# One store of the result from every 16th partition, behind the closing barriers of a decode kernel

## The chip, the cores and the metric

The kernel runs on one core of a Trainium2 chip. The metric is the time of one execution on the device, in microseconds (us). It is given as the median of three runs, and one more execution, which the hardware profiler recorded, gives the trace. The trace has the core's engines: TensorE (PE, and PEld for its weight loads), VectorE (DVE), ScalarE (ACT), GpSimd (POOL) and SyncE (SP), and 16 DMA engines that carry all transfers between HBM and the on-chip memory.

## What is computed

The kernel mixes two branches for two tokens (batch 2, one position each, model width 512). Branch A is attention of one new position over the last 4,096 positions of a cache, with 32 query heads that share 8 key and value heads of width 128. Branch B is a dense layer of 1,792 units with the Mish activation. A sigmoid gate weighs the two.

```python
W = min(4096, max(256, Sk // 4))                       # 4096
q = (x @ wq).reshape(B, Sq, Hq, Dh)                    # 2 tokens, 32 heads of 128
scores = einsum("bhqd,bhkd->bhqk", q, k[last W]) * Dh ** -0.5
a = einsum("bhqk,bhkd->bhqd", softmax(scores), v[last W]).reshape(B, Sq, Hq * Dh) @ wo
h = x @ w1 + b1
b = (h * tanh(softplus(h))) @ w2
g = sigmoid((x * gate_w).sum(-1, keepdims=True))
return g * a + (1 - g) * b                             # (2, 1, 512), float32
```

All inputs and the output are float32.

## The kernel before

Everything is read once: the query weights (two loads of 4 MB), `w1`, then for each of the 8 key heads a block of keys and a block of values (4 MB each), then `w2` and `wo` in pieces. All loads are issued from SP's queue, in one fixed order; the big ones take turns in five buffers of the pool `stream`, so that a load waits until the buffer of the fifth load before it is free.

With only two tokens, a plain matrix product would use two rows of the output. The kernel instead divides the 128 partitions of a PSUM tile into 4 blocks of `Q = 32` rows. The inputs of a matmul are padded to 32 columns (`x32`, `oT`, `actT`: the two tokens are columns 0 and 1, the other 30 are zero), and block `j` of the output takes another slice of the weights. So a result tile holds, in partition `32 * j + b`, slice `j` of token `b`; the other partitions hold zeros.

- `queries` (from line 107) makes the queries of four key heads each, transposes them, and copies the two tokens' columns into `qz` (16 copies, listed in the profile under line 122).
- `hidden` (line 202) makes the hidden layer, adds the bias while it reads the transposed tile (line 227), and writes the activations, weighted by one minus the gate, into the token columns of `actT` (line 242).
- `softmax` and `values` (lines 126 and 145) go over the key heads; `weights` and `outputs` (lines 158 and 193) scale what the heads gave and write it into the token columns of `oT` (line 198).
- `project` and `finish` (lines 276 and 285) multiply by `wo` and `w2`. The last sum is in the PSUM tile `fin`, of 128 x 128: partition `32 * j + b` has the columns `128 j` to `128 j + 127` of token `b`'s output.

At the end VectorE copies `fin` to `res` in SBUF (line 319), and two stores write the result, one for each token: SP issues the one for token 0 and ScalarE the one for token 1, each from the four partitions `b`, `b + 32`, `b + 64` and `b + 96`.

The kernel is written within a tile context (`with tile.TileContext`, line 360), which places the tiles and sets every semaphore wait. When the context closes, it adds an ending of its own, which the profile lists under line 360: SP waits for the semaphores of all DMAs and engines that the context knows; then all engines meet in a barrier that GpSimd leads; GpSimd drains and clears the context's semaphores; and a second barrier follows, which is the end of the program.

Of the kernel before, what the change touches and what calls it, by code (L numbers as in the profile page):

```python
# [8 lines left out]
F32 = mybir.dt.float32  # L9
# [4 lines left out]
P = 128  # L14
B = 2
D = 512
HQ = 32
HKV = 8
REP = HQ // HKV
# [5 lines left out]
NJ = 4  # L25
NT = 4
Q = 32
BH = B * REP
F = 1792
DC = D // P  # L30
FC = F // P
FG = 4
# [5 lines left out]


@with_exitstack  # L40
def decode_kernel(ctx: ExitStack, tc: tile.TileContext, small, wq, kt, v, wo, w1, w2, out):
    nc = tc.nc

    const = ctx.enter_context(tc.tile_pool(name="const", bufs=1))
# [14 lines left out]
    xT = sm[:, : DC * B].rearrange("p (c b) -> p c b", b=B)  # L59
# [6 lines left out]
    make_identity(nc, ident)  # L66
    fold = const.tile([P, Q], F32, name="fold")
    nc.vector.tensor_reduce(fold, ident.rearrange("p (j r) -> p r j", r=Q), axis=AX.X, op=ALU.add)
    key = const.tile([P, B, REP], F32, name="key")
    fv = fold.rearrange("p (y n h) -> p y n h", n=NH, h=REP)  # L70
    nc.vector.tensor_tensor(key, fv[:, :B, 0, :], fv[:, :B, 1, :], op=ALU.add)
    pick = const.tile([P, Q // REP], F32, name="pick")
    nc.vector.tensor_reduce(pick, fold.rearrange("p (m h) -> p m h", h=REP), axis=AX.X, op=ALU.add)
    ones = const.tile([P, P], F32, name="ones")
    nc.vector.memset(ones, 1.0)

    x32 = const.tile([P, DC, Q], F32, name="x32")
    nc.vector.memset(x32, 0.0)
    nc.vector.tensor_copy(x32[:, :, :B], xT)  # L79
    qz = const.tile([P, HKV, BN * (Q + REP)], F32, name="qz")  # L80
    nc.gpsimd.memset(qz, 0.0)
    oT = const.tile([P, HQ, Q], F32, name="oT")
    nc.gpsimd.memset(oT, 0.0)
    actT = const.tile([P, FC, Q], F32, name="actT")
# [5 lines left out]
    def gates():  # L90
        xg = const.tile([P, DC, B], F32, name="xg")
        nc.vector.tensor_tensor(xg, xT, gw[:, :, None].to_broadcast([P, DC, B]), op=ALU.mult)
        xs = const.tile([P, B], F32, name="xs")
        nc.vector.tensor_reduce(xs, xg.rearrange("p c b -> p b c"), axis=AX.X, op=ALU.add)
        zp = ps_1.tile([P, B], F32, tag="q", name="zp")
        nc.tensor.matmul(zp, ones, xs, start=True, stop=True)  # L96
        g = const.tile([P, B], F32, name="g")
        omg = const.tile([P, B], F32, name="omg")
        nc.scalar.activation(g, zp, AF.Exp, scale=-1.0)
        nc.vector.tensor_scalar_add(g, g, 1.0)  # L100
        nc.vector.reciprocal(g, g)
        nc.vector.tensor_scalar(omg, g, -1.0, 1.0, op0=ALU.mult, op1=ALU.add)
        return g, omg

    g, omg = gates()

    def queries(i, t):
        w = t.rearrange("p (c k n) -> p c k n", c=DC, k=HALF)
        qp = ps_1.tile([P, REP * DH], F32, tag="o", name=f"qp{i}")
        for c in range(DC):  # L110
            for k in range(HALF):
                nc.tensor.matmul(qp[Q * k : Q * k + Q, :], x32[:, c, :], w[:, c, k, :],  # L112
                                 start=(c == 0), stop=(c == DC - 1))
        qs = work.tile([P, REP * DH], F32, tag="p", name=f"qs{i}")
        nc.vector.tensor_copy(qs, qp)
        qt = ps_1.tile([P, REP, HALF, Q], F32, tag="pt", name=f"qt{i}")
        for h in range(REP):
            nc.tensor.transpose(qt[:, h].rearrange("p k r -> p (k r)"),
                                qs[:, h * DH : (h + 1) * DH], ident)
        for k in range(HALF):  # L120
            for n in range(NH):
                nc.vector.tensor_copy(
                    qz[:, i * HALF + k, :].rearrange("p (b n x) -> p b n x", n=NH, x=Q + REP)[:, :, n, :REP],
                    qt[:, :, k, :B].rearrange("p h b -> p b h"))

    def softmax(kv, t):
        sc = ps_s.tile([P, 512], F32, tag="sc", name=f"sc{kv}")
# [30 lines left out]
    def weights():  # L158
# [19 lines left out]
        nc.vector.tensor_tensor(fl, fs, ls, op=ALU.mult)  # L178
        kf = const.tile([P, HKV, BH], F32, name="kf")
        kl = const.tile([P, HKV, BH], F32, name="kl")  # L180
        kb = key.rearrange("p b h -> p (b h)")[:, None, :].to_broadcast([P, HKV, BH])
        nc.vector.tensor_tensor(kl, kb, fl[:, :, None].to_broadcast([P, HKV, BH]), op=ALU.mult)
        nc.vector.tensor_tensor(kf, kb, fs[:, :, None].to_broadcast([P, HKV, BH]), op=ALU.mult)
        lp = ps_1.tile([P, HKV, B, REP], F32, tag="q", name="lp")
# [8 lines left out]
    def outputs(ol, kf, r, k0, k1):  # L193
        for kv in range(k0, k1):
            nc.tensor.matmul(ol[:, kv].rearrange("p b h -> p (b h)"), od[:, kv, :], kf[:, kv, :],  # L195
                             start=True, stop=True)
        for b in range(B):
            nc.vector.tensor_tensor(
                oT.rearrange("p (k h) x -> p k h x", h=REP)[:, k0:k1, :, b],
                ol[:, k0:k1, b, :], r[:, k0:k1, b, :], op=ALU.mult)  # L200

    def hidden(t):
        w = t[:, : DC * F].rearrange("p (c f) -> p c f", c=DC)
        hp = ps_1.tile([P, FG * P], F32, tag="o", name="hp")
        for c in range(DC):
            for j in range(NJ):
                n = min(FG, FC - j * FG) * P
                nc.tensor.matmul(hp[Q * j : Q * j + Q, :n], x32[:, c, :],  # L208
                                 w[:, c, j * FG * P : j * FG * P + n],
                                 start=(c == 0), stop=(c == DC - 1))  # L210
        hs = work.tile([P, FG * P], F32, tag="p", name="hs")
        nl = (FC - (NJ - 1) * FG) * P
        nc.vector.tensor_copy(hs[:, :nl], hp[:, :nl])
        nc.vector.tensor_copy(hs[: Q * (NJ - 1), nl:], hp[: Q * (NJ - 1), nl:])
        ht = ps_1.tile([P, FG, NJ, Q], F32, tag="pt", name="ht")

        def m(name):
            return const.tile([P, FC, B], F32, name=name)

        h, e, e2, s, wt, nu = (m(x) for x in ("h", "e", "e2", "s", "wt", "nu"))  # L220
        for k in range(FG):
            nj = len(range(k, FC, FG))
            nc.tensor.transpose(ht[:, k, :nj, :].rearrange("p j r -> p (j r)"),
                                hs[: Q * nj, k * P : (k + 1) * P], ident[: Q * nj, : Q * nj])
        for k in range(FG):
            nj = len(range(k, FC, FG))
            nc.vector.tensor_tensor(h[:, k::FG, :], ht[:, k, :nj, :B],
                                    b1[:, k::FG, None].to_broadcast([P, nj, B]), op=ALU.add)
        nc.vector.scalar_tensor_tensor(e, h, -1.0, h, op0=ALU.mult, op1=ALU.max)
        nc.scalar.activation(e, e, AF.Exp, scale=-1.0)  # L230
        nc.vector.tensor_scalar(s, h, 0.0, None, op0=ALU.is_gt)
        nc.vector.tensor_tensor(e2, e, e, op=ALU.mult)
        nc.vector.tensor_scalar(wt, e2, -1.0, 1.0, op0=ALU.mult, op1=ALU.add)
        nc.vector.tensor_tensor(wt, wt, s, op=ALU.mult)
        nc.vector.tensor_tensor(wt, wt, e2, op=ALU.add)
        nc.vector.scalar_tensor_tensor(nu, e, 2.0, wt, op0=ALU.mult, op1=ALU.add)
        nc.vector.scalar_tensor_tensor(wt, e2, 1.0, wt, op0=ALU.add, op1=ALU.subtract)
        nc.vector.scalar_tensor_tensor(wt, wt, 2.0, nu, op0=ALU.mult, op1=ALU.add)
        nc.vector.reciprocal(wt, wt)
        nc.vector.tensor_tensor(nu, nu, wt, op=ALU.mult)  # L240
        nc.vector.tensor_tensor(nu, nu, h, op=ALU.mult)
        nc.vector.tensor_tensor(actT[:, :, :B], nu, omg[:, None, :].to_broadcast([P, FC, B]),
                                op=ALU.mult)

    queries(0, wq_a)
    queries(1, wq_b)
    hidden(w1_t)

    for kv in range(HKV - 1):
# [23 lines left out]
    fin = ps_1.tile([P, P], F32, tag="fin", name="fin")  # L273
# [18 lines left out]
    kf, r = weights()  # L292
    ol = ps_1.tile([P, HKV, B, REP], F32, tag="q", name="ol")
    outputs(ol, kf, r, 0, HKV - 1)
    values(HKV - 1, pT, last_v)
    for f in range(CUTS[1]):
        project(f % NJ, actT[:, f, :], w2_0[:, f * D : (f + 1) * D], n_of[f % NJ])
    outputs(ol, kf, r, HKV - 1, HKV)
    for k0, k1, t in wos:
        for kv in range(k0, k1):  # L300
            for h in range(REP):
                x = ((kv - k0) * REP + h) * D
# [12 lines left out]
    output(2)  # L315
    output(3)

    res = const.tile([P, P], F32, name="res")
    nc.vector.tensor_copy(res, fin)
    for b, eng in enumerate((nc.sync, nc.scalar)):  # L320
        eng.dma_start(out[b].rearrange("s (j n) -> (s j) n", n=P), res[b::Q, :])


# [40 lines left out]
```

## Time and profile before

| | us |
|---|---|
| three runs | 221.21, 222.17, 222.28 |
| their median | 222.17 |
| the profiled execution | 221.15 |
| its span, from the first to the last instruction | 219.4 |

| engine | busy us | share of the span |
|---|---|---|
| PE | 130.3 | 59% |
| PEld | 38.4 | 18% |
| DVE | 36.2 | 17% |
| ACT | 8.6 | 4% |
| POOL | 3.0 | 1% |

The loads bring 91.24 MB from HBM, 416 GB/s over the span. The mean granted clock of TensorE was 0.805 of full speed.

In the page of the profile, times are microseconds and the mean of one instruction is in nanoseconds. An arrow `out<-in` names what an instruction writes and reads; `<-` behind an idle time names what ended it. The chain that ended last is followed back from the last instruction to whatever released each step. An engine's name with a `q` (SPq, POOLq) is its sequencer: semaphore waits, drains and DMA issues stand there, and they are not counted as busy. The view of one source line gives, for each kind of instruction, the count, the shortest, median and longest duration, and the first and last start. A table of windows gives, for each stretch, its length, the busy time of PE, PEld, DVE, ACT and POOL, the granted clock, the share of the 16 DMA engines that was busy and the GB/s that they moved.

### The profile page before, as it was taken

What the parts mean: (1) busy time and instruction counts of PE and PEld (TensorE: products, weight loads), DVE (VectorE), ACT (ScalarE), POOL (GpSimd) and SP (SyncE); (2) the same over time, 40 slices, a digit from 0 to 9 for tenths busy, and PEclk for the clock granted to TensorE, in tenths of its full rate; (3) what the DMA queues carried; (4) which work ended last, traced back from release to release, by engine and by line L of the source; (5) the groups of instructions that cost most, each with busy time, mean ns of one, the idle gap of its engine ahead of it and who ended that gap; (6) DMA issues with size and microseconds to landing.
All of it is one profiled execution on the core that took longest, in us unless ns stands there. A gap on an engine that the chain in (4) does not pass through costs nothing.

```text
span 219.4 us, 1884 instructions
## 1 busy us (share of the span) xinstructions
PE 130.3 (59%) x798; PEld 38.4 (18%) x798; DVE 36.2 (17%) x131; ACT 8.6 (4%) x21; POOL 3.0 (1%) x9
## 2 busy tenths in 40 slices
PE   0058838376175927556493948648284756497763
PEld 0011312112011201212120221112011111341211
DVE  1011211511202011120202021020211103502001
ACT  2000000001001000000100010010001001000000
POOL 5000000000000000000000000000000000000000
PEclk9999976679958788887857576696966757859999
DMA  7898999999999999999999999999999999999990
GB/s 287 388 474 388 455 418 457 424 432 448 412 454 406 469 388 466 406 460 400 457 406 460 418 442 430 430 448 409 466 394 466 394 466 415 436 413 421 423 393 34
DMA packets 4055, 91.35 MB, mean 416 GB/s; under 512 B 584, under 2 KB 592, under 8 KB 976
## 3 DMA queue, kind: packets, MB, share of 16 engines
q1 hardware_dynamic: 4040, 91.24, 96.9%
q8 instruction: 6, 0.10, 0.2%
q14 instruction: 1, 0.01, 0.0%
q10 hardware_dynamic: 8, 0.00, 0.0%
HBM read 91.24 MB, written 0.00 MB: 416 GB/s over the span
## 4 chain that ended last, share of the span: by engine, by line
DMA 69%; PE 24%; DVE 3%; ACT 1%; issue 1%; SPq 0%; ACTq 0%; DVEq 0%
DMA k<-in_kt 57%; PE sc L130 9%; PE o L149 8%; DMA w<-in_w 7%; DMA sm<-in_small 5%; PE qp L112 3%; PE ol L195 1%; ACT p L137 1%; DVE mx L133 1%; DVE pT L142 1%; PE pp L141 1%; PE fin L287 1%; SPq L53 0%; DVE r L188 0%; PE zp L96 0%
## 5 line engine op out<-in xcount | busy, mean ns | idle before, releaser
L130 PE MATMUL sc<-k,qz 128*32 128x512 f32 x256 | 45.8, 882 | 33.1 <-DMA k<-in_kt 33.1
L149 PE MATMUL o<-v,pT 128*32 128x512 f32 x256 | 43.1, 834 | 10.4 <-DMA v<-in_v 8.7
L130 PEld LDWEIGHTS sc<-k,qz 128*32 128x32 f32 x256 | 10.4, 155 | 67.8 <-DMA k<-in_kt 39.9
L149 PEld LDWEIGHTS o<-v,pT 128*32 128x32 f32 x256 | 11.4, 146 | 36.5 <-issue 28.8
L133 DVE TENSOR_REDUCE mx<-sc 128x1 f32<-128x512 f32 x8 | 5.5, 692 | 64.9 <-PE sc L130 64.9
L112 PE MATMUL qp<-wqa,x 128*32 128x512 f32 x32 | 7.3, 870 | 13.4 <-DVE x L79 13.4
L141 PE MATMUL pp<-ident,p 128*128 128x128 f32 x32 | 5.5, 297 | 14.4 <-ACT p L137 14.4
L137 ACT ACTIVATE p<-sc,bias 128x512 f32<-128x512 f32 x8 | 5.5, 687 | 140.2 <-DVE bias L135 120.6
L153 DVE TENSOR_SCALAR od<-o,pick 128x128 f32<-128x128 f32 x8 | 2.8, 351 | 48.5 <-PE o L149 48.5
L277 PE MATMUL acc<-wo,oT 128*32 128x512 f32 x64 | 7.7, 597 | 3.2 <-DMA wo<-in_wo 3.2
L155 DVE SCALAR_TENSOR_TENSOR od<-o,pick,od 128x128 f32<-128x128 f32 x24 | 8.4, 351 | 0.8
L208 PE MATMUL hp<-w,x 128*32 128x512 f32 (+1 forms) x32 | 6.2, 863 | 3.4 <-DMA w<-in_w 3.4
L142 DVE COPY pT<-pp 128x512 f32<-128x512 f32 x8 | 5.5, 692 | 11.8 <-PE pp L141 11.7
L141 PEld LDWEIGHTS pp<-ident,p 128*128 128x128 f32 x32 | 3.4, 140 | 21.2 <-ACT p L137 21.2
L195 PE MATMUL ol<-kf,od 128*128 128x8 f32 x16 | 3.5, 350 | 2.3 <-DVE od L155 1.6
L112 PEld LDWEIGHTS qp<-wqa,x 128*32 128x32 f32 x32 | 1.4, 152 | 16.7 <-DVE x L79 13.4
L195 PEld LDWEIGHTS ol<-kf,od 128*128 128x128 f32 x16 | 3.4, 312 | 3.3 <-DVE od L155 2.5
L112 PE MATMUL qp<-wqb,x 128*32 128x512 f32 x32 | 3.6, 594 | 0.1
L277 PEld LDWEIGHTS acc<-wo,oT 128*32 128x32 f32 x64 | 1.7, 109 | 9.0 <-issue 4.7
L208 PEld LDWEIGHTS hp<-w,x 128*32 128x32 f32 x32 | 1.7, 158 | 7.2 <-issue 7.2
L277 PE MATMUL acc<-w,actT 128*32 128x512 f32 x20 | 2.8, 597 | 0.0
L306 DVE COPY asum<-acc 128x256 f32<-128x256 f32 x1 | 0.4, 425 | 13.6 <-ACT asum L305 13.6
(75 smaller groups left out, 32.5 us busy)
## 6 DMA issues: line engine op xcount, KB each, us to landing
k<-in_kt SPq DMA_DIRECT2D x8, 4096.0 KB, 42.5
v<-in_v SPq DMA_DIRECT2D x8, 4096.0 KB, 42.8
wqa<-in_wq SPq DMA_DIRECT2D x1, 4096.0 KB, 12.2
wqb<-in_wq SPq DMA_DIRECT2D x1, 4096.0 KB, 21.0
wo<-in_wo SPq DMA_DIRECT2D x1, 4096.0 KB
w<-in_w SPq DMA_DIRECT2D x1, 3584.0 KB, 29.1
w<-in_w SPq DMA_DIRECT2D x1, 2560.0 KB
wo<-in_wo SPq DMA_DIRECT2D x1, 2048.0 KB, 33.9
```

The source lines that it names most:

```text
L112: nc.tensor.matmul(qp[Q * k : Q * k + Q, :], x32[:, c, :], w[:, c, k, :], start=(c == 0), stop=(c == DC - 1))
L130: nc.tensor.matmul(sc[Q * j : Q * j + Q, :], qz[:, kv, m * Q : m * Q + Q], t[:, (m * NJ + j) * 512 : (m * NJ + j + 1) * 512], start=(m == ...
L133: nc.vector.tensor_reduce(mx[:, kv : kv + 1], sc, axis=AX.X, op=ALU.max)
L137: nc.scalar.activation(p, sc, AF.Exp, bias=bias, scale=SCALE, accum_out=ls[:, kv : kv + 1])
L141: nc.tensor.transpose(pp[:, c, :], p[:, c * P : (c + 1) * P], ident)
L142: nc.vector.tensor_copy(pT, pp)
L149: nc.tensor.matmul(o[Q * j : Q * j + Q], pT[:, c, Q * j : Q * j + Q], t[:, (c * NJ + j) * 512 : (c * NJ + j + 1) * 512], start=(c == 0), s ...
L153: nc.vector.tensor_scalar_mul(d, o[:, 0, :], pick[:, 0:1])
L155: nc.vector.scalar_tensor_tensor(d, o[:, m, :], pick[:, m : m + 1], d, op0=ALU.mult, op1=ALU.add)
L195: nc.tensor.matmul(ol[:, kv].rearrange("p b h -> p (b h)"), od[:, kv, :], kf[:, kv, :], start=True, stop=True)
L208: nc.tensor.matmul(hp[Q * j : Q * j + Q, :n], x32[:, c, :], w[:, c, j * FG * P : j * FG * P + n], start=(c == 0), stop=(c == DC - 1))
L277: nc.tensor.matmul(acc[Q * j : Q * j + Q, :], lhsT, rhs, start=(n_col[j] == 0), stop=(n_col[j] == n - 1))
```

## The change

The two tokens move from columns 0 and 1 of each block of 32 to columns 0 and 16 (`RS = Q // B = 16`). Each place that writes or reads the token columns takes a step of 16. In `fin` and `res` the eight rows of the result then lie in partitions 0, 16, 32 and so on to 112, and one DMA from SP stores them all. The output in HBM becomes a matrix of 8 x 128, whose rows are ordered by slice and then token; the host puts them in the reference's order after the run.

`res` is no longer a tile of the pool `const` but a tensor of its own, and the store carries a semaphore of its own, `stored`, instead of one of the tile context (`no_tile_sem_insts`). The dependence of the store on the copy is given by hand. Behind the tile context, so behind its two closing barriers, GpSimd waits until `stored` is 16, and then clears and frees that semaphore. ScalarE issues no store any more.

```diff
+RS = Q // B
...
-    nc.vector.tensor_copy(x32[:, :, :B], xT)
+    nc.vector.tensor_copy(x32[:, :, ::RS], xT)
...
-                    qt[:, :, k, :B].rearrange("p h b -> p b h"))
+                    qt[:, :, k, ::RS].rearrange("p h b -> p b h"))
...
-                oT.rearrange("p (k h) x -> p k h x", h=REP)[:, k0:k1, :, b],
+                oT.rearrange("p (k h) x -> p k h x", h=REP)[:, k0:k1, :, b * RS],
...
-            nc.vector.tensor_tensor(h[:, k::FG, :], ht[:, k, :nj, :B],
+            nc.vector.tensor_tensor(h[:, k::FG, :], ht[:, k, :nj, ::RS],
...
-        nc.vector.tensor_tensor(actT[:, :, :B], nu, omg[:, None, :].to_broadcast([P, FC, B]),
+        nc.vector.tensor_tensor(actT[:, :, ::RS], nu, omg[:, None, :].to_broadcast([P, FC, B]),
...
-    res = const.tile([P, P], F32, name="res")
-    nc.vector.tensor_copy(res, fin)
-    for b, eng in enumerate((nc.sync, nc.scalar)):
-        eng.dma_start(out[b].rearrange("s (j n) -> (s j) n", n=P), res[b::Q, :])
+    copy = nc.vector.tensor_copy(res, fin)
+    store = nc.sync.dma_start(out, res[::RS, :]).then_inc(stored, 16)
+    tc.no_tile_sem_insts.add(store.ins.name)
+    tc.add_manual_dep(store.ins, copy.ins.name,
+                      mybir.DependencyInfo(mybir.DependencyClass.Sync, mybir.DependencyReason.DATA),
+                      reason="the store reads the copy")
...
-    args.append(nc.dram_tensor("out_0", (B, 1, D), F32, kind="ExternalOutput").ap())
+    args.append(nc.dram_tensor("out_0", (NJ * B, P), F32, kind="ExternalOutput").ap())
+    stored = nc.alloc_semaphore("stored")
+    res = nc.alloc_sbuf_tensor("res", [P, P], F32).ap()
     with tile.TileContext(nc) as tc:
-        decode_kernel(tc, *args)
+        decode_kernel(tc, res, stored, *args)
+    nc.gpsimd.wait_ge(stored, 16)
+    nc.clear_and_free_semaphores([stored])
...
-    return r.results[0]["out_0"]
+    return r.results[0]["out_0"].reshape(NJ, B, P).transpose(1, 0, 2).reshape(B, 1, D)
```

More of the change, by code (lines that the diff above doesn't have):

```diff
@@ L40, in decode_kernel @@
 @with_exitstack
-def decode_kernel(ctx: ExitStack, tc: tile.TileContext, small, wq, kt, v, wo, w1, w2, out):
+def decode_kernel(ctx: ExitStack, tc: tile.TileContext, res, stored, small, wq, kt, v, wo, w1, w2, out):
     nc = tc.nc
```

## The prediction

> **What bounds the kernel now.** I read the page's head first, then the chain that ended last, then the end in ever finer views, because all that the change does to the order of work lies behind the last matmul.
>
> ```profile
> span 219.4 us, 1884 instructions
> ...
> DMA  7898999999999999999999999999999999999990
> ...
> q1 hardware_dynamic: 4040, 91.24, 96.9%
> ...
> q10 hardware_dynamic: 8, 0.00, 0.0%
> ```
>
> The 16 DMA engines are busy from the first slice to the last but one: queue q1 (SP's) carries 91.24 MB in 96.9% of the span. Over nearly the whole span, then, the loads set the pace, and a few nanoseconds on another engine disappear behind them. Queue q10 (ScalarE's) has 8 packets: that is one of the two stores, of four rows.
>
> The chain in order of time shows where this cover ends:
>
> ```profile
> 199.21 15.04 DMA w<-in_w
> 214.25 0.04 issue
> 214.30 1.79 PE fin L287 x40
> 216.09 0.02 issue
> 216.11 0.29 DVE res L319
> ```
>
> From 214.25 on nothing is loaded that anything waits for long: last matmuls, copy out of PSUM, stores. The copy ends at 216.40, and 3.0 us of the span still follow. The timeline of that stretch has only the issues of the stores:
>
> ```profile
> 216.43 0.62 SPq L321 DMA_DIRECT2D out<-res  x1
> 216.43 1.33 ACTq L321 DMA_DIRECT2D out<-res  x1
> ```
>
> The waits of SP's queue in the last four microseconds name what it does then:
>
> ```profile
> SPq L321 <- DVE res L319: 13.2, 1, 13.2
> SPq L360 <- DMA out<-res: 1.2, 1, 1.2
> SPq L360 <- PEq L360: 0.6, 2, 0.4
> ```
>
> Line 360 opens and closes the tile context. There SP waits until every DMA has landed, 1.2 us for a store, and only then do the engines meet in two barriers. The view of line 360 from 216 us on, row by row (columns: count, shortest, median and longest ns, first and last start):
>
> ```profile
> L360 SPq EVENT_SEMAPHORE  x7: 17/28/28, 217.1 to 219.3; - x7
> L360 POOLq EVENT_SEMAPHORE  x4: 17/17/17, 218.7 to 219.3; - x4
> ...
> L360 ACTq DRAIN  x2: 8/82/157, 217.8 to 218.9; - x2
> ...
> L360 PEldq EVENT_SEMAPHORE  x2: 51/51/51, 218.8 to 219.3; - x2
> L360 POOLq DRAIN  x2: 34/56/78, 218.9 to 219.1; - x2
> L360 POOLq EVENT_SEMAPHORE_RANGE_CLEAR  x1: 96/96/96, 219.0 to 219.0; - x1
> ```
>
> SP's first closing wait starts at 217.1, right behind its store's issue (216.43 + 0.62 = 217.05). GpSimd gathers at 218.7, releases all engines at 218.8, drains and clears semaphores from 218.9 to 219.1, and releases them again at 219.3; PE's 51 ns instruction ends the span. So the end is strictly in series: issue, landing of the slower store, barriers.
>
> **The change part by part.**
>
> *The wait that goes.* The new store carries no semaphore of the tile context, so SP's closing waits no longer include it; the other DMAs that they name landed long before. SP still issues first (0.62 us by its own row), starts its waits at 217.1 and runs straight through. The whole 1.2 us go from the barriers: the last instruction of the second one moves from 219.4 to 218.2, GpSimd's own last one from 219.3 to 218.1. Does another engine come late instead? ScalarE's drain was at 217.8, behind its 1.33 us issue, which is removed; before the copy it has only its half of `asum`, so it is early. DVE and PE have nothing behind the copy, which ends at 216.40. GpSimd has had nothing since the head. SP stays the last to arrive, and the gain here is the full 1.2.
>
> *The store itself.* When does one store of eight rows land? Fine windows of the old stores show it (last columns: DMA share and GB/s):
>
> ```profile
> 216.43:217.64 1.21, 0.00 (x0) 0.00 (x0) 0.00 (x0) 0.00 (x0) 0.00 (x0) 1.00 0.00 0
> 217.64:217.76 0.12, 0.00 (x0) 0.00 (x0) 0.00 (x0) 0.00 (x0) 0.00 (x0) 1.00 0.07 17
> 217.76:217.92 0.16, 0.00 (x0) 0.00 (x0) 0.00 (x0) 0.00 (x0) 0.00 (x0) 1.00 0.00 0
> 217.92:218.04 0.12, 0.00 (x0) 0.00 (x0) 0.00 (x0) 0.00 (x0) 0.00 (x0) 1.00 0.07 17
> ```
>
> 17 GB/s for 0.12 us are 2 KB: one store at 217.7, the other at 218.0. The first I take as SP's, whose issue ended first. SP was released at 217.1 + 0.03 + 1.2, about 218.35, so a store counts as landed some 0.35 us behind its packets. SP's own thus landed at about 217.75 + 0.35 = 218.1, 1.67 us behind the start of its issue, and the other at 218.35, 1.92 behind. For the eight-row store on SP I take 218.1, the row of the same queue. Bounds: below, the first load of the kernel, which met an idle queue:
>
> ```profile
> 0.73 0.38 SPq L53 DMA_DIRECT2D wqa<-in_wq  x1
> ```
>
> It took 0.38 us to issue; with no second store beside it the new one might do likewise, 0.24 earlier, landing at 217.85. Above, ScalarE's 218.35; and if the issue grows with the rows, 0.62 / 4 = 0.156 us each, the issue lasts 1.25 and both the landing and SP's waits come 0.62 later.
>
> The Trainium skill's page "DMA: Bandwidth & Descriptors", section "Anatomy of one DMA", puts the fixed part of a DMA at about 2.0 us, nearly all of it the receipt, heaviest for HBM. That is a rule against this change, since a wait for the receipt remains; here the two stores took 1.67 and 1.92, less than it says. By 2.0 an estimate has the store landed at 218.43 and the gain at 0.65; the sum goes by the rows.
>
> *The wait and the clear that are added.* They come behind the barriers on GpSimd. Queued behind the wait on that engine is only the clear, and no other engine waits for either. GpSimd is free at 218.1, the store is landed at 218.1: two events at nearly one time, so the wait itself costs little. Then the clear, whose like stands at line 360: a drain (78 ns) and a range clear (96 ns), from the drain's start at 218.9 to the next drain's start at 219.1, 0.2 us; with the wait instruction in front about 0.3. GpSimd ends at 218.4. The tail lies beside nothing. Bounds: 0.2 (the clear without its drain's spacing) to 0.55 (the same, with the store landed at 218.35).
>
> *The rest.* The new strides change no count and no tile shape. Their instructions and a pair that prices strides:
>
> ```profile
> L122 DVE COPY qz<-qt 128x8 f32<-128x8 f32 x16 | 1.4, 157 | 1.6 <-PE qt L118 1.6
> L68 DVE TENSOR_REDUCE fold<-ident 128x32 f32<-128x128 f32 x1 | 0.4, 371 | 1.1 <-POOL ident masks.py:199 1.1
> L227 DVE TENSOR_TENSOR h<-ht,sm 128x8 f32<-128x8 f32 x2 | 0.2, 162 | 0.5 <-PE ht L223 0.5
> L227 DVE TENSOR_TENSOR h<-ht,sm 128x6 f32<-128x6 f32 x2 | 0.2, 156 | 0.0
> L242 DVE TENSOR_TENSOR actT<-nu,omg 128x28 f32<-128x28 f32 x1 | 0.2, 189 | 0.1
> L79 DVE COPY x<-sm 128x8 f32<-128x8 f32 x1 | 0.2, 173 | 10.2 <-DMA sm<-in_small 10.2
> L73 DVE TENSOR_REDUCE pick<-fold 128x8 f32<-128x32 f32 x1 | 0.2, 177 | 0.0
> ```
>
> L68 reads 128 elements per partition at a step of 32, L73 reads 32 in order: 194 ns for 96 more elements, at most 2 ns each if all of it were for the stride. So 8 elements cost 0 to 16 ns more, and all of it, 16 x 16 at L122, four at L227, L79 and 28 elements at L242, at most 0.26 + 0.06 + 0.02 + 0.06 = 0.4 us, spread over the first fifth of the span. I take nothing: the loads above cover it, and without that cover it would be those 0.4. The write at line 198 had a step of 32 and keeps it. Below zero: nothing is taken out. `res` outside the pools adds no instruction.
>
> *The sum.* Span 219.4 - 1.2 + about 0.2 (GpSimd's 218.4 against the barriers' 218.2) = 218.4. The profiled execution took 221.15, that is 1.75 outside the span, which I leave as it is: 220.15, a gain of 1.0. That execution is the fastest shown; the three runs have 221.21, 222.17 and 222.28. From their median the forecast is 222.17 - 1.0 = 221.2 us. No run here shows what the 1.75 consist of. The Trainium skill's page "Runtime: NRT & Kernel Launch", section on the preamble and postamble, has a barrier of all engines behind every kernel; by it GpSimd's late end counts in full, as in the sum, and a GpSimd that isn't last in that barrier could hide it.
>
> **The rivals.**
>
> *More gain, 1.2 or above.* Either the 0.24 of a load-like issue comes off both the barriers and the landing (span 218.15, gain 1.25), or what follows the span hides GpSimd's 0.2 (gain 1.2): 220.9 to 221.0. For it: ScalarE's issue lasts 1.33 beside SP's 0.62 though both start at 216.43, as if they shared something, and with one store nothing is shared. Against: SP began first and still needed more than the load's 0.38.
>
> *Less, because rows cost.* Issue 1.25: waits from 217.7, barriers to 218.8, landed 218.7, end 219.0, gain 0.4: 221.8. For it: four rows took longer than the load. Against: that load has 128 partitions and took 0.38, so rows are not what an issue pays for.
>
> *Nothing.* What ends the measured time is not the last engine but something fixed behind it, and the 1.75 grow by what the span loses: 222.2. The stores' landing at 218.1 to 218.35 would have to be what counts. Against: the engines' last instruction comes a full 1.0 behind the later landing, and the 1.75 more behind that instruction would have to know of it.
>
> *Slower.* One mechanism: the issue pays per row at ScalarE's price, 1.33 / 4 = 0.33, eight rows 2.66. SP's issue then ends at 219.09, the store lands 1.05 behind that (as SP's did behind 217.05) at 220.15, and the clear ends at 220.45, 1.05 later than now: 223.2. It decides from a landing later than 219.4 - 0.3 = 219.1, which is 2.67 us behind the start of the issue, against 1.67 and 1.92 seen. The load's 0.38 speaks against it.
>
> **How the numbers follow.** Forecast (gain 0.75 to 1.1) 0.45; more 0.28; less 0.12; nothing 0.09; slower 0.06. A measurement can tell about 0.5%, 1.1 us, from no change, and the runs before lie 1.07 apart. "More" counts as faster, and of the forecast, whose upper end lies at that limit, about three in ten by that scatter: 0.28 + 0.14 = 0.42. Slower over 0.5%: most of the slower rival and a little scatter from "nothing": 0.06. Within: 0.52. The range: low, the lowest run less the largest gain, 221.21 - 1.25 = 220.0; high, 222.2, which takes in "less" and reaches the median with no gain. The forecast's own range about the median is 221.1 to 221.4.
>
> **What would show it.** Right: SP's wait for `out<-res` at the close is gone, q10 is gone and q1 has 4,048 packets (eight more), GpSimd's last clear is the end of the span at 218.4 if the copy again ends at 216.40 (2.0 behind the copy instead of 3.0), with the other engines done 0.2 before. Wrong: an SP issue far from 0.62, a landing far from 1.67 behind it, or a time outside the span that is not 1.75. The forecast fails as a whole if GpSimd's wait is long, for then the store is again in series with the end.

## The result and the profile after

| | median us | runs | ratio to the kernel before, 95% interval |
|---|---|---|---|
| before, beside it | 222.16 | 6 (221.01 to 222.28) | |
| changed | 220.28 | 6 (220.15 to 220.39) | 0.9944 (0.9922 to 0.9967) |
| before, second comparison | 221.34 | 18 (221.04 to 222.38) | |
| changed, second comparison | 220.38 | 6 (220.13 to 220.45) | 0.9948 (0.9928 to 0.9967) |

The changed kernel is faster: by about half a per cent in the ratios, by some 0.4% where like runs are compared. One thing must be known to read the medians: the runs of most kernels in this study lie in two groups some 1.1 us apart, and the spans differ by the same amount. In the first comparison four of the six runs of the kernel before were in its upper group, in the second three of eighteen. So the difference of the first two medians, 1.88, is not the gain. Without the upper group the medians of the second comparison are 221.30 and 220.38, 0.92 apart. The two profiled executions, both of a lower group, took 221.15 and 220.15.

The head of the changed kernel's page:

```profile
span 218.3 us, 1883 instructions
...
q1 hardware_dynamic: 4048, 91.25, 97.4%
```

The loads fill the span as before; q10 is gone and q1 has the eight packets more. The end, in the changed kernel's timeline (start, length):

```profile
215.96 0.29 DVE L319 COPY res<-fin 128x128 f32<-128x128 f32 x1 [0.97 <-PE fin L288]
216.28 0.70 SPq L320 DMA_DIRECT2D out<-res  x1
```

The waits of SP's queue in the last microseconds of the changed kernel:

```profile
SPq L320 <- DVE res L319: 15.6, 1, 15.6
SPq L365 <- PEq L365: 0.6, 2, 0.4
```

SP's 1.2 us for the store at the close are gone. The closing of the tile context (now line 365) and GpSimd's clear behind it (line 368) have these rows (count, shortest, median and longest ns, first and last start):

```profile
L365 SPq EVENT_SEMAPHORE  x7: 17/28/28, 217.0 to 218.1; - x7
L365 POOLq EVENT_SEMAPHORE  x4: 17/17/17, 217.5 to 218.1; - x4
L365 SPq DRAIN  x3: 7/7/90, 217.4 to 217.8; - x3
...
L365 PEldq EVENT_SEMAPHORE  x2: 51/51/51, 217.7 to 218.1; - x2
```

```profile
L368 POOLq DRAIN  x1: 60/60/60, 218.2 to 218.2; - x1
L368 POOLq EVENT_SEMAPHORE_RANGE_CLEAR  x1: 44/44/44, 218.3 to 218.3; - x1
```

GpSimd gathers the engines at 217.5, 1.3 behind the copy's end at 215.96 + 0.29 = 216.25; before it was 218.7 against 216.40, 2.3 behind. Its own last barrier instruction is at 218.1 and the drain of its clear at 218.2: within what the view resolves it didn't wait for the store. (The wait has no row of its own; it can only be read from the gap ahead of that drain.) Fine windows show why:

```profile
216.28:217.56 1.28, 0.00 (x0) 0.00 (x0) 0.00 (x0) 0.00 (x0) 0.00 (x0) 1.00 0.00 0
217.56:217.68 0.12, 0.00 (x0) 0.00 (x0) 0.00 (x0) 0.00 (x0) 0.00 (x0) 1.00 0.15 34
```

34 GB/s for 0.12 us are the 4 KB of the eight rows, at 217.6; 0.35 behind that the store has landed, at about 218.0.

When the copy ends scatters from run to run with the load stream. To compare endings I therefore use one figure below: the time of the profiled execution less the end of the copy to `res`. It is 221.15 - 216.40 = 4.75 for the kernel before and 220.15 - 216.25 = 3.90 for the changed one. So 0.85 of the 1.00 between the two executions is the ending, and 0.15 is a copy that happened to end earlier. The figure comes from one execution of each kernel and leaves out whatever a change does ahead of that copy; a table behind the experiments sets it beside the medians of all runs.

### The profile page after: what moved, and what is told of

Read it like the earlier page. It is cut to its first block, busy times and chain, and to the rows that moved or that the text cites. A ratio compares the mean times of both kernels' runs of the same rounds, so it can differ in the third digit from the quotient of the medians.

```text
span 218.3 us, 1883 instructions
## 1 busy us (share of the span) xinstructions
PE 132.7 (61%) x798; PEld 39.3 (18%) x798; DVE 36.2 (17%) x131; ACT 8.6 (4%) x21; POOL 3.0 (1%) x9
## 4 chain that ended last, share of the span: by engine, by line
DMA 70%; PE 24%; DVE 3%; ACT 1%; issue 1%; SPq 0%; ACTq 0%; DVEq 0%
DMA k<-in_kt 57%; PE sc L131 9%; PE o L150 8%; DMA w<-in_w 7%; DMA sm<-in_small 6%; PE qp L113 3%; PE ol L196 1%; ACT p L138 1%; DVE mx L134 1%; DVE pT L143 1%; PE pp L142 1%; PE fin L288 1%; SPq L54 0%; PE lp L186 0%; DVE r L189 0%
## 5 line engine op out<-in xcount | busy, mean ns | idle before, releaser
L150 PE MATMUL o<-v,pT 128*32 128x512 f32 x256 | 45.7, 879 | 10.8 <-DMA v<-in_v 9.3
L278 PEld LDWEIGHTS acc<-wo,oT 128*32 128x32 f32 x64 | 2.4, 109 | 8.1 <-issue 4.3
L116 DVE COPY qs<-qp 128x512 f32<-128x512 f32 x2 | 1.4, 692 | 7.8 <-PE qp L113 7.8
```

The source lines that it names most:

```text
L150: nc.tensor.matmul(o[Q * j : Q * j + Q], pT[:, c, Q * j : Q * j + Q], t[:, (c * NJ + j) * 512 : (c * NJ + j + 1) * 512], start=(c == 0), s ...
L278: nc.tensor.matmul(acc[Q * j : Q * j + Q, :], lhsT, rhs, start=(n_col[j] == 0), stop=(n_col[j] == n - 1))
```

## The experiments

The theory was that the gain is the store's landing taken out from in front of the barriers. The first rival was that it is one store instead of two.

**The kernel before once more,** with no edit.

> The kernel before, unchanged, for the scatter of its runs and their spans. So far its runs lie in two groups, 221.0 to 221.2 and 222.2 to 222.3, while all six of the changed kernel lie within 220.15 to 220.39. If the two groups are a property of the load stream, the spans will differ by the same 1.1 us (219.3 and 220.4) and the time outside the span stays 1.75 to 1.8 in both. If they come from what follows the last instruction, the spans agree within 0.2 and the time outside the span differs by 1.1.

Median 221.25 of 12 runs. The copy in its profiled execution (221.15 us):

```profile
216.08 0.29 DVE L319 COPY res<-fin 128x128 f32<-128x128 f32 x1 [0.99 <-PE fin L287]
```

221.15 - 216.37 = 4.78, against 4.75: the figure repeats within 0.03, and I take 4.77 for the kernel before. Ten runs lie within 221.04 to 221.49, two at 222.06 and 222.51, with spans of 220.3 and 220.7 against 219.2 to 219.7. So the difference between the groups lies inside the span. That it comes from the load stream and not from the end is likely but not shown, since no profiled execution of this kernel was in the upper group.

**The strides alone.** The five places that write or read the token columns take the step of 16 as in the changed kernel, and the stores become

```diff
-        eng.dma_start(out[b].rearrange("s (j n) -> (s j) n", n=P), res[b::Q, :])
+        eng.dma_start(out[b].rearrange("s (j n) -> (s j) n", n=P), res[b * RS::Q, :])
```

> Only the token columns move to 0 and 16; two stores as before, by the tile context's semaphores. Theory (the gain is the store's landing taken out of the way of the barriers): nothing changes, span of the profile 219.4 within 0.1 and time 221.15 or 222.2, in the two groups of the kernel before. Rival (the layout itself is what keeps the changed kernel's runs out of the upper group): all runs within 221.0 to 221.3.

Median 221.34 of 12, ratio 1.0001 (0.9981 to 1.0020), three runs in an upper group. Its profiled execution took 221.16 us:

```profile
216.07 0.29 DVE L320 COPY res<-fin 128x128 f32<-128x128 f32 x1 [1.02 <-PE fin L288]
```

Figure 221.16 - 216.36 = 4.80: the ending is the same. What the strides cost ahead of the copy stands in the rows of the strided instructions (count, shortest, median and longest ns):

```profile
L123 DVE COPY qz<-qt x16: 155/156/167, 22.9 to 28.5; 128x8 f32<-128x8 f32 x16
L243 DVE TENSOR_TENSOR actT<-nu,omg x1: 207/207/207, 42.2 to 42.2; 128x28 f32<-128x28 f32 x1
```

The 16 copies take what they took before (157 ns on average), and the write of `actT` takes 18 ns more than its 189. The layout changes nothing that the time shows, and it doesn't take the upper group away.

**One store, but SP waits for it.**

```diff
-    store = nc.sync.dma_start(out, res[::RS, :]).then_inc(stored, 16)
+    nc.sync.dma_start(out, res[::RS, :])
...
-    nc.gpsimd.wait_ge(stored, 16)
-    nc.clear_and_free_semaphores([stored])
```

> One store out of every 16th partition, but with the tile context's own semaphore, so that SP's closing wait includes it and nothing follows the barriers. Theory (overlap): the store lands 1.72 behind its issue's start instead of the later store's 1.91, so 0.2 us of gain, span 219.2, and SP's wait for the store stays at about 1.0. Rival (one store instead of two is the gain, ScalarE's second store being what made the end late): the full 1.0, span 218.4.

Median 221.06 of 12, ratio 0.9999 (0.9981 to 1.0017). From the timeline and the waits of the profiled execution (221.01 us):

```profile
216.17 0.29 DVE L320 COPY res<-fin 128x128 f32<-128x128 f32 x1 [1.01 <-PE fin L288]
216.49 0.69 SPq L321 DMA_DIRECT2D out<-res  x1
```

```profile
SPq L360 <- DMA out<-res: 0.9, 1, 0.9
```

SP waits 0.9 instead of 1.2, and the figure is 221.01 - 216.46 = 4.55: a gain of 0.22, as the theory had it. (The ratio mixes the two groups and shows no change; the medians of the lower groups differ by 0.16.) The rival, that one store is the whole gain, falls. The wait also shows a landing that the changed kernel hides: issue 216.49 + 0.69, the next instruction some 0.06 behind, 0.9 of wait, so about 218.2, 1.7 behind the start of the issue.

**Two stores, both waited for late.**

```diff
-        eng.dma_start(out[b].rearrange("s (j n) -> (s j) n", n=P), res[b::Q, :])
+        store = eng.dma_start(out[b].rearrange("s (j n) -> (s j) n", n=P),
+                              res[b::Q, :]).then_inc(stored[b], 16)
+        tc.no_tile_sem_insts.add(store.ins.name)
...
+    for s in stored:
+        nc.gpsimd.wait_ge(s, 16)
+    nc.clear_and_free_semaphores(stored)
```

> The layout and the two stores of before, each store with a semaphore of its own that GpSimd waits for behind the barriers. Theory (overlap): ScalarE's issue (1.33) and drain (0.16) end at 217.96 and are now the last arrival at the first barrier instead of SP's 218.67, so the barriers end 0.7 earlier, at 218.65; the later store has landed at 218.34 by then, two waits and the clear add 0.2 to 0.3, span 218.9, a gain of 0.5. Rival (one store instead of two is the gain): no gain, span 219.4.

Median 220.78 of 12, ratio 0.9984 (0.9967 to 1.0001). The profiled execution took 220.81 us; its copy, and the rows of line 366, the closing:

```profile
216.20 0.29 DVE L318 COPY res<-fin 128x128 f32<-128x128 f32 x1 [0.96 <-PE fin L287]
```

```profile
L366 POOLq EVENT_SEMAPHORE  x4: 17/17/17, 218.1 to 218.6; - x4
L366 SPq DRAIN  x3: 7/7/277, 217.5 to 218.3; - x3
...
L366 ACTq DRAIN  x2: 8/82/157, 217.9 to 218.3; - x2
```

Figure 220.81 - 216.49 = 4.32, a gain of 0.45, as the theory had it; the medians of the lower groups differ by 0.43. GpSimd gathers at 218.1, 1.6 behind the copy's end, right behind ScalarE's drain (217.9 + 0.16). So ScalarE's store held the first barrier here. The late wait and the single store are worth 0.45 and 0.22 apart and 0.87 together: each takes away something that stands in the way of the other.

**The store from ScalarE.**

```diff
-    store = nc.sync.dma_start(out, res[::RS, :]).then_inc(stored, 16)
+    store = nc.scalar.dma_start(out, res[::RS, :]).then_inc(stored, 16)
```

> The changed kernel with its one store issued by ScalarE, so that SP's closing waits start early and ScalarE's drain is the last arrival at the first barrier. Theory (the 1.33 us of ScalarE's issue in the kernel before came from the second store beside it): the issue takes about 0.70 as on SP, its drain ends some 1.2 behind the issue's start as SP's did, the first barrier gathers within 0.1 of the changed kernel's 1.29 behind the copy's end, and the end comes 2.0 to 2.1 behind the copy's end, as now. Rival (ScalarE issues slowly by itself): issue 1.33 or more, gather at about 1.7, end at 2.4 behind the copy.

Median 220.53 of 8, ratio 0.9957 (0.9942 to 0.9972). The profiled execution (220.56 us):

```profile
216.23 0.29 DVE L319 COPY res<-fin 128x128 f32<-128x128 f32 x1 [1.01 <-PE fin L288]
216.55 1.16 ACTq L320 DMA_DIRECT2D out<-res  x1
```

```profile
L365 POOLq EVENT_SEMAPHORE  x4: 17/17/17, 217.9 to 218.5; - x4
```

The issue took 1.16 us with no other store beside it: nearer to the rival's 1.33 than to the theory's 0.70. ScalarE is slower than SP at issuing this store, by itself. The gather comes 217.9 - 216.52 = 1.4 behind the copy's end, though, nearer to the theory's 1.29 than to the rival's 1.7, and the span ends 2.2 behind it, between the theory's 2.1 and the rival's 2.4: so neither holds as a whole. The figure is 220.56 - 216.52 = 4.04, 0.14 worse than from SP.

**No clear.**

```diff
     nc.gpsimd.wait_ge(stored, 16)
-    nc.clear_and_free_semaphores([stored])
```

> The changed kernel without the clearing of its own semaphore; GpSimd still waits for the store. Theory (GpSimd is the last engine, and what follows the span waits for it): GpSimd ends at once behind its wait, 0.10 to 0.13 earlier, and the time falls by as much, to 220.05 in the lower group. Rival (GpSimd's tail lies beside what follows the span): the span shrinks by 0.1 and the time stays.

Median 220.34 of 11, three of them in an upper group, ratio 0.9959 (0.9940 to 0.9977). The profiled execution took 220.07 us:

```profile
215.99 0.29 DVE L319 COPY res<-fin 128x128 f32<-128x128 f32 x1 [0.97 <-PE fin L288]
```

Figure 220.07 - 216.28 = 3.79, 0.11 less than the changed kernel. That is the clear's 60 + 44 ns, in full, and the rival, that the time stays, falls: what follows the span does wait for GpSimd.

**SP waits, no clear.**

```diff
-    nc.gpsimd.wait_ge(stored, 16)
-    nc.clear_and_free_semaphores([stored])
+    nc.sync.wait_ge(stored, 16)
```

> The changed kernel with SP instead of GpSimd waiting for the store behind the barriers, and without the clear. GpSimd then ends with the second barrier, 0.21 before its present end, and SP ends some 0.06 behind its last barrier instruction. Theory (what follows the span waits for GpSimd above all): time 0.2 less than the changed kernel, more than the span shows (0.1). Rival (it waits for the last engine, whichever it is): as in the kernel without the clear, 0.1 less in both.

Median 220.18 of 6, ratio 0.9940 (0.9921 to 0.9960); profiled execution 220.32 us:

```profile
216.26 0.29 DVE L319 COPY res<-fin 128x128 f32<-128x128 f32 x1 [1.02 <-PE fin L288]
```

Figure 220.32 - 216.55 = 3.77, 0.13 less than the changed kernel and 0.02 less than with GpSimd's wait and no clear. The theory's 0.2 is not reached by this figure, but the medians of the lower groups, from the same comparison, differ by 0.20, and over all runs the time less the span has a mean of 1.76 here and 1.84 in the changed kernel. So the time fell by more than the span, as the theory had it and the rival did not; how much of the 0.2 is there, six runs don't settle.

**The changed kernel once more,** with no edit.

> The changed kernel, unchanged, beside many runs of the kernel before on one chip. Theory: its runs have the same two groups as all the others (about one in five in the upper one, some 1.1 higher), the lower groups differ by 0.9, the ratio is 0.996, and the 0.9944 of the first comparison came from a draw with four of six runs of the kernel before in its upper group. Rival (the change also takes the upper group away): no run above 220.9 in twelve, ratio 0.994 to 0.995.

Its row is in the table of the result; the profiled execution took 220.13 us:

```profile
215.94 0.29 DVE L319 COPY res<-fin 128x128 f32<-128x128 f32 x1 [1.04 <-PE fin L288]
```

220.13 - 216.23 = 3.90, the same as the first time. Taken by itself the rival's sign came true: six more runs, none in an upper group. But the kernel without the clear, whose program is the same up to the closing barriers, had three of eleven there, and the 16-row kernel below four of twelve. I take it for chance and not for a gain; twelve runs are too few to settle it.

**A store of 16 rows.** The output becomes 16 x 128, and the host drops the rows of zeros in between.

```diff
-    store = nc.sync.dma_start(out, res[::RS, :]).then_inc(stored, 16)
+    store = nc.sync.dma_start(out, res[:: RS // 2, :]).then_inc(stored, 16)
```

> The changed kernel with a store of 16 rows, every eighth partition, of which the rows in between hold zeros that the host drops. It tests what SP's issue of a store pays for: 4 rows took 0.63 us, 8 rows 0.70, loads of 128 rows 0.38 to 0.53. Theory (rows do not count; a store that doesn't spread over all 16 DMA engines pays extra): issue 0.4 to 0.5, SP's drain 7 ns instead of 90, so the first barrier gathers 0.25 to 0.35 earlier, at about 1.0 behind the copy's end instead of 1.29; the store lands at most 0.2 earlier and GpSimd's wait is now what ends last; end 1.85 behind the copy's end instead of 2.07. Rival (each row costs): issue 0.8 or more, end 2.15 or later behind the copy.

Median 220.25 of 12, ratio 0.9965 (0.9946 to 0.9983). Timeline and closing (line 365) of the profiled execution, 220.09 us:

```profile
216.04 0.29 DVE L319 COPY res<-fin 128x128 f32<-128x128 f32 x1 [1.00 <-PE fin L288]
216.36 0.56 SPq L320 DMA_DIRECT2D out<-res  x1
```

```profile
L365 POOLq EVENT_SEMAPHORE  x4: 17/17/17, 217.4 to 218.0; - x4
L365 SPq DRAIN  x3: 7/7/38, 217.3 to 217.6; - x3
```

Twice the rows take less to issue, 0.56 against 0.70, and SP's drain 38 ns against 90. So an issue does not pay by rows. The theory's 0.4 to 0.5 and 7 ns were not reached either; what an issue pays for stays open. The figure is 220.09 - 216.33 = 3.76, a gain of 0.14 where the theory had 0.22. The gather came 0.20 earlier behind the copy than in the changed kernel (1.09 against 1.29), but the landing did not (the store's last packet ends 1.41 behind the copy in both), and now it shows: in the trace GpSimd's last barrier instruction starts at 217.97 and the drain of the clear at 218.11, 0.14 later, where the changed kernel has 218.09 and 218.19, 0.10. So GpSimd waits some 0.04 for the store here.

**16 rows, SP waits, no clear:** the two edits together.

> The 16-row store with SP instead of GpSimd waiting for it, and without the clear: the two gains together, if both hold. Theory: 0.2 to 0.3 below the changed kernel, lower group at 220.0 to 220.1. Rival (the landing now ends last and moves neither with the wait nor with the issue): no more than 0.13 below it, as with SP's wait alone.

Median 220.16 of 12 (219.85 to 221.15), ratio 0.9949 (0.9930 to 0.9969), with four runs in an upper group. Profiled execution 220.27 us, with a late copy:

```profile
216.44 0.29 DVE L319 COPY res<-fin 128x128 f32<-128x128 f32 x1 [1.01 <-PE fin L288]
```

Figure 220.27 - 216.73 = 3.54, 0.36 below the changed kernel: more than 0.13 + 0.14 and more than the rival allows; by the medians of the lower groups it is 0.26 (table), as the theory had it. It has the shortest ending of all. Its eight runs of the lower group have a median of 220.02, the changed kernel's twelve runs one of 220.34. A direct comparison of the two beside each other was not made.

**A store that lands late: a failed pair.** Two kernels got a store of 1 MB of zeros to a scratch tensor, meant to land behind the barriers, with the late wait in one and with SP's wait in the other.

```diff
+    extra = nc.scalar.dma_start(scratch, big).then_inc(more, 16)
...
+    nc.gpsimd.wait_ge(more, 16)
```

> The changed kernel and a second store of 1 MB of zeros to a scratch tensor, issued by ScalarE behind its half of asum, so that it lands later than the result, I estimate at 218.6 on the scale of the changed kernel; GpSimd waits for both behind the barriers. Theory: the barriers don't move (SP and ScalarE are done with issuing by then), and the end follows the landing by 0.15 to 0.25. So the overlap is worth the same whatever the landing, as long as it falls behind the barriers.

> The same extra store and the one store of the result, both with the tile context's semaphores, so that SP waits for both ahead of the barriers. Theory: the end follows the last landing by 1.0, as in the kernel before (218.34 to 219.36), so this kernel ends 0.8 later than the one that waits late. Rival (a late landing makes the two alike, since both end with a wait): within 0.3 of each other.

The first took 224.48 (median of 4, ratio 1.0132, 1.0096 to 1.0168), the second 224.98 (1.0159, 1.0128 to 1.0189). The view of the scratch tensor in the first kernel, and its copy:

```profile
L311 ACTq DMA_DIRECT2D scratch<-big x1: 336/336/336, 5.3 to 5.3; - x1
```

```profile
220.02 0.29 DVE L327 COPY res<-fin 128x128 f32<-128x128 f32 x1 [0.97 <-PE fin L290]
```

The extra store depended only on a fill at the start, and the tile context placed it there, at 5.3 us. It ran beside the first loads (the small one landed 15.6 us behind its issue instead of 12.0, and the copy ends at 220.31 instead of 216.25) and had long landed at the end, 11.3 us behind its own issue. So neither expectation was tested. What remains is one more pair of endings: the first took 224.28 in its profiled execution, 3.97 behind the copy (3.90 and a second semaphore to wait for), the second, with SP waiting first, 4.48 (copy's end 219.96, time 224.44). How the two ways compare when a store lands far behind the barriers stays open.

**The endings side by side.** The lower group of a kernel are its runs within 0.8 us of its fastest. The gain by medians is the lower group's median against that of the kernel before in the same comparison; the last column is the mean, over all runs, of the time less the span.

| | time less the copy's end | gain | gain by medians | outside the span |
|---|---|---|---|---|
| before | 4.77 | | | 1.79 |
| strides alone | 4.80 | -0.03 | -0.12 | 1.79 |
| one store, SP waits first | 4.55 | 0.22 | 0.16 | 1.80 |
| two stores, waited for late | 4.32 | 0.45 | 0.43 | 1.85 |
| one late store from ScalarE | 4.04 | 0.73 | 0.77 | 1.85 |
| changed | 3.90 | 0.87 | 0.92 | 1.84 |
| no clear | 3.79 | 0.98 | 1.08 | 1.87 |
| SP waits, no clear | 3.77 | 1.00 | 1.12 | 1.76 |
| 16 rows | 3.76 | 1.01 | 1.03 | 1.84 |
| 16 rows, SP waits, no clear | 3.54 | 1.23 | 1.18 | 1.77 |

The two gains agree within 0.12, so the single executions are fair samples. The last column is not constant: it is 1.84 to 1.87 wherever GpSimd's instruction is the last, 1.79 to 1.80 where TensorE's is, and 1.76 to 1.77 where SP's is. Why, no run shows.

## Why the prediction was right, and where it was off

**The mechanism: right.** A single chain was cut at SP's wait. With the wait in front of the barriers, one store gives 0.22; with it behind them, 0.87.

**"The whole 1.2 us go from the barriers": 1.0.** The gather moved from 2.3 to 1.3 behind the copy's end. The step that failed is that SP "starts its waits at 217.1 and runs straight through" with an issue of 0.62. The issue of eight rows took 0.70, and SP's drain, which had taken 7 ns when the store had already landed, took 90. These are 0.16 of the 0.2 that lack.

**The tail: 0.2 forecast, 0.1 measured.** In the trace the last barrier instruction ends at 218.20 and the clear, with which the span ends, at 218.32, and removing the clear took 0.11 off the time. The clear of one semaphore took 60 + 44 ns and not the 78 + 96 of the context's. The two errors cancel in part: 1.2 - 0.2 = 1.0 was forecast, 0.87 is the measured gain of the ending, between its bounds of 0.75 and 1.1.

**The landing: right,** 1.67 forecast, 1.7 measured where SP still waits for it. GpSimd and the landing do meet within 0.1. The Trainium skill's page "DMA: Bandwidth & Descriptors" gives its about 2.0 us, in the section "Anatomy of one DMA", for DMAs that GpSimd issues, and this store goes out from SP. An estimate by it has the store landed at 216.28 + 2.0 = 218.28 and GpSimd waiting some 0.1 for it; the drain of the clear, which starts at 218.2, shows no such wait.

**Outside the span: not quite as assumed.** The prediction left this part as it was. Over all runs it has a mean of 1.79 before and 1.84 in the changed kernel, so some 0.05 of what the span gains is lost behind it. With the other two parts that closes the sum: 1.0 from the barriers, less 0.12 for the tail, less 0.05, comes to 0.83, against the 0.85 of the two profiled executions. The rival that something hides GpSimd's tail falls by the kernel without the clear and its 0.11. The Trainium skill's page "Runtime: NRT & Kernel Launch", in its section on the preamble and postamble, has a barrier of all engines behind a kernel; the 0.11 agree with it.

**The strides: right,** nothing that the time shows: 18 ns at the write of `actT`, and a ratio of 1.0001 for the strides alone, which leaves room for up to 0.4 us either way.

**The rivals.** "More" by a shorter issue fell: SP alone needed 0.70. Its reason, that the two issues shared something, is at most a small part, since ScalarE alone still took 1.16 (for eight rows; four rows from ScalarE alone were not run). Neither 0.156 nor 0.33 per row holds, since 8 rows took 0.70 and 16 rows 0.56; with that "less" and "slower" are gone. "Nothing" fell with the result.

**The number.** From the profiled execution the sum gave 220.15, and the changed kernel's took 220.15. That is chance: the ending gained 0.85 and not 1.0, and a copy that ended 0.15 earlier made up for it. The forecast of 221.2 came from subtracting the gain from a median of three, two of which were in the upper group. That step was wrong: the measured 220.28 lies 0.9 below it, below the forecast's own 221.1 to 221.4 and even below the 220.9 of the rival with more gain. It lies within the whole range only because the low end of that, 220.0, was reckoned from the lowest run. The wrong step also hid that the likeliest case, within 0.5%, lay at the edge: 0.87 of 221.15 is 0.4%, and the measured ratios, 0.9944 and 0.9948, are just beyond 0.5%, with intervals that reach from 0.3% to 0.8%.

## What to carry to other kernels

A store of the result at the end of a kernel need not land before the closing barriers, only before the program ends: given a semaphore of its own and waited for behind them, its landing and the barriers run side by side. Look then at which engine arrives last at the first barrier, since a second store on a queue that issues slowly takes back part of the gain. And when a change touches only the end, measure from the last instruction that it leaves alone: here that repeated to 0.03 us where medians moved by 1. Set it beside the medians of like runs, because it can show nothing of what the change does ahead of that instruction.

## What the hardware showed that I had not expected

- A drain on SP's queue behind a store just issued is not free: 90 ns (8 rows), 277 (4 rows, with ScalarE's store beside it), 38 (16 rows), against 7 where SP had waited for the store first. It doesn't wait for the landing: in the changed kernel it ends at 217.4 + 0.09, and the store's packets move only at 217.6.
- An issue's length follows neither rows nor bytes: stores of 4, 8 and 16 rows took 0.63, 0.70 and 0.56 us on SP. ScalarE took 1.33 for 4 rows beside SP's store and 1.16 for 8 rows alone.
- The time outside the span differs with the engine that ends last: 1.84 to 1.87 us with GpSimd, 1.79 to 1.80 with TensorE, 1.76 to 1.77 with SP.
- Runs of one program differ by 1.1 us in the span in about one case in five. What makes a run take the longer course was not tried.
